# Cached attention decode on one core: the ring of tile slots moved to a multiple of 4096 bytes in each partition

## The chip, the cores and the metric

The kernel runs on one core of one Trainium2 chip. The metric is the device time of one execution in microseconds (us), the median of several runs. A profile belongs to one execution of its own; its span runs from the first to the last instruction.

## The reference

Two independent attention blocks, A and B, each decode one token against a cache; the outputs are put side by side.

```python
B, Sq, D = 8, 1, 1024
H, Sk, Dh = 32, 4096, 128
...
def _A_ref(x, k_cache, v_cache, wq, wo):
    q = (x @ wq).reshape(B, Sq, H, Dh).transpose(0, 2, 1, 3)
    scores = jnp.einsum("bhqd,bhkd->bhqk", q, k_cache) * (Dh ** -0.5)
    p = _softmax(scores, axis=-1)
    o = jnp.einsum("bhqk,bhkd->bhqd", p, v_cache)
    return o.transpose(0, 2, 1, 3).reshape(B, Sq, H * Dh) @ wo
...
return jnp.concatenate([a, b], axis=-1)
```

All is bfloat16. A cache of one block is 8 x 32 x 4096 x 128 numbers, 268 MB, and there are four: K and V of A and of B. Each number of a cache is used once.

## The kernel before, in words

The on-chip memory has 128 partitions. The kernel cuts each cache into tiles of 8 heads of one batch (`HQ = 8`): 8 x 4096 x 128 numbers, 8 MiB. A tile lies in the partitions as 128 rows of 65,536 bytes: each head has 16 partitions, and each partition 256 positions of 128 numbers (`T = 256`, `Dh = 128`). A block has 32 K tiles and 32 V tiles, so `NQ = 64` pairs of a K and a V tile in all. The weights wq and wo of a block are 8 MiB each and travel as tiles too.

**The ring.** `ring` (line 191) is one tensor of three tile slots, 3 x 65,536 bytes in each partition. The list `plan` (lines 271 to 275) says in which order the tiles are loaded and into which slot. K tiles take slots 0 and 1 in turn, V tiles take slot 2. A block's wq goes through slots 1 and 2; the last V tile and the two wo tiles use what is free. `load_tiles` (line 291) issues each load on SyncE's queue (SP) as soon as the operation that last used the slot has been issued to its engine; SP then waits on the chip for that operation to end (line 241 for cache tiles, line 233 for weights). The last wo comes in four pieces (`wo_cuts`, line 223: 20, 8, 3 and 1 of 32 heads' columns), so that the projection can begin on the first. The two inputs x are put into the start of slot 2 (line 479) by ScalarE's queue.

**The work on a K tile.** In four chunks of 64 positions (`CT = 64`, `NR = 4`): VectorE (DVE) multiplies the chunk in place by the query, which lies in `qbc` for all partitions (line 362); it adds the upper 64 numbers of each position to the lower 64 (line 367); TensorE adds four groups of 16 by matmuls with the identity `ident` (line 377) into PSUM; VectorE adds the last 16 into `s_sb` (line 385). After the fourth chunk come the maximum (lines 391 to 395), the exponential on ScalarE (line 397) into `pe`, and line 402, which spreads the probabilities over 8 columns (`PM`), of which each partition fills the one of its head.

**The work on a V tile.** TensorE multiplies `PM` with the V tile (line 414), 64 matmuls, half of them in the third and half in the fourth chunk of the next K tile. ScalarE copies the sum to `accS` (line 422), TensorE picks out the heads (line 431), and ScalarE stores them in `o_sb` (line 437). At the end come the division by the sums (line 451) and the two projections with wo (line 467), a copy (line 474) and the output.

**The order of the work.** It is written out by hand: each engine has a list of operations, filled by the loop at line 498, and each operation names what it waits for. Each `sb(...)` at lines 191 to 212 allocates a tensor in every partition; they lie one behind another in the order of these lines. Ahead of them lie four one-element constants that the framework allocates. Sizes per partition that matter here: `s_sb` 2 x 256 x 4 = 2048 bytes, `accS` 512 x 2 = 1024, `qst` 2 x 128 x 2 = 512, `ident` 128 x 2 = 256, `own_m` 8 x 4 x 4 = 128.

Of the kernel before, what the change touches and what calls it, by code (L numbers as in the profile page):

```python
# [8 lines left out]
BF16 = mybir.dt.bfloat16  # L9
FP32 = mybir.dt.float32  # L10
# [154 lines left out]
def _build_kernel(nc, caches, out):  # L165
    B, Sq, D = caches[0][0].shape
    _, H, Sk, Dh = caches[0][1].shape
# [6 lines left out]
    T = Sk // MP  # L174
# [12 lines left out]
    with es:  # L187
        sb = lambda name, shape, dt: es.enter_context(nc.sbuf_tensor(name, shape, dt))
        ps = lambda name, n=512: es.enter_context(nc.psum_tensor(name, [128, n], FP32))

        ring = sb("ring", [128, 3, T * Dh], BF16)
        ident = sb("ident", [128, 128], BF16)
        own_m = sb("own_m", [128, HQ, PH], FP32)
        own_h = sb("own_h", [128, HQ], BF16)
        half = sb("half", [128, 2], FP32)
        E = sb("E", [128, 4, MB + PH - 1], BF16)
        xT = sb("xT", [128, NC * DC * B], BF16)
        qT = sb("qT", [128, NC, H * B], BF16)
        qst = sb("qst", [128, 2, 128], BF16)
        qbc = sb("qbc", [128, 2, Dh], BF16)  # L200
        s_sb = sb("s_sb", [128, 2, T], FP32)
        rmax = sb("rmax", [128, 1], FP32)
        rtmp = sb("rtmp", [128, 32], FP32)
        ngm = sb("ngm", [128, 2], FP32)
        rsum = sb("rsum", [128, NQ], FP32)
        pe = sb("pe", [128, T], BF16)
        PM = sb("PM", [128, T, HQ], BF16)
        accS = sb("accS", [128, 512], BF16)
        o_sb = sb("o_sb", [128, NC * B * H], FP32)
        rl = sb("rl", [128, B], FP32)  # L210
        on_sb = sb("on_sb", [128, NC, B * H + H], BF16)
# [360 lines left out]
def bass_concat_heads__mha_block_cached__mha_block_cached__decode_kernel(  # L572
    nc, A_x, A_k_cache, A_v_cache, A_wq, A_wo, B_x, B_k_cache, B_v_cache, B_wq, B_wo, out,
):
    caches = [(A_x, A_k_cache, A_v_cache, A_wq, A_wo), (B_x, B_k_cache, B_v_cache, B_wq, B_wo)]
    _build_kernel(nc, caches, out)
# [28 lines left out]
```

## Time and profile before

| | us |
|---|---|
| median of 3 runs | 2563.58 (2563.41 to 2563.61) |
| span of the profiled execution | 2562.3 |
| DVE busy | 2170.4 (85%) |
| PE matmul busy | 1116.5 (44%) |
| ACT busy | 129.9 (5%) |
| time that the packets of the SP queue took, as a share of 16 DMA engines' span | 99.9% |

The profiled execution has its span beside no time of its own; it is 1.3 us below the median of the runs. PE is TensorE, PEld its weight loads, DVE VectorE, ACT ScalarE, POOL GpSimd, SP SyncE; SPq is SP's queue of DMA issues. A group row of the profile reads: line, engine, operation, output<-inputs, shapes, count, then busy time and mean ns of one, then the idle time of the engine ahead of it and what ended it. A row of the timeline reads: start and duration in us, engine, line, operation, and in brackets the idle time ahead of it with its releaser. A row of a tile's view gives the shortest, median and longest duration in ns. A row of waits gives the total, the count and the longest. A row of DMA issues gives the count, the size where it is one, and the time from issue to landing in us. A row of windows gives the stretch, its length, the busy time of PE, PEld, DVE, ACT and POOL with the count of instructions, TensorE's granted clock, the DMA engines' share and GB/s.

### The profile page before, as it was taken

The page shows a single profiled execution, that of the slowest core. Times are in us where ns is not written, and L with a number is a line of the kernel's source. Part 1 is how long each engine was busy: PE and PEld are TensorE (multiplying, and loading weights), DVE is VectorE, ACT ScalarE, POOL GpSimd, SP SyncE. Part 2 cuts the span into 40 slices and gives each one's busy share as a digit, 9 for nine tenths or more (in the row PEclk, how much of TensorE's full clock was granted, in tenths as well). Part 3 has the DMA queues.
Part 4 walks back from the last instruction along what each step waited for, and adds up shares of the span by engine and source line. Part 5 has one row for each costly group of instructions (what it writes and reads, how often), then busy time and mean ns, then how long its engine had stood idle before and what let it go on. Part 6 is the DMA issues. An engine that isn't in the chain of part 4 may idle for free.

```text
span 2562.3 us, 18889 instructions
## 1 busy us (share of the span) xinstructions
PE 1116.5 (44%) x7712; PEld 397.0 (15%) x7712; DVE 2170.4 (85%) x1042; ACT 129.9 (5%) x401; POOL 2.6 (0%) x15
## 2 busy tenths in 40 slices
PE   2443443443444444444434444444434434434434
PEld 0111111111111111111111111111111111111112
DVE  3898898898898898898898888988988988988983
ACT  1100000000000000000000000000000000000000
POOL 0000000000000000000000000000000000000000
PEclk8666676766767677767767767766767667666667
DMA  9999999999999999999999999999999999999999
GB/s 425 427 438 430 438 430 438 430 438 430 437 430 437 429 436 431 435 433 433 435 432 436 431 436 431 437 431 437 431 437 431 437 431 437 431 435 433 435 433 394
DMA packets 19552, 1107.49 MB, mean 432 GB/s; under 512 B 2184, under 2 KB 2248, under 8 KB 2520
## 3 DMA queue, kind: packets, MB, share of 16 engines
q1 hardware_dynamic: 19512, 1107.34, 99.9%
q8 instruction: 7, 0.11, 0.0%
q10 hardware_dynamic: 32, 0.03, 0.0%
q14 instruction: 1, 0.01, 0.0%
HBM read 1107.33 MB, written 0.03 MB: 432 GB/s over the span
## 4 chain that ended last, share of the span: by engine, by line
DMA 52%; DVE 28%; issue 16%; PE 4%; ACT 0%; another core or an unknown queue 0%; DVEq 0%; SPq 0%
DMA ring<-in_A_k_cache_dram 25%; DMA ring<-in_B_k_cache_dram 25%; DVE ring L362 10%; DVE ring L367 10%; PE red L377 4%; DVE s_sb L385 4%; DVE PM L402 3%; DMA ring<-in_B_wo_dram 2%; DVE rmax L391 1%; DVE rtmp L392 0%; ACT PM L323 0%; PE o L317 0%; DVEq L161 0%; DVE ngm L395 0%
## 5 line engine op out<-in xcount | busy, mean ns | idle before, releaser
L362 DVE TENSOR_TENSOR ring<-ring,qbc 128x8192 bf16<-128x8192 bf16 x256 | 1131.4, 4420 | 309.8 <-DMA ring<-in_A_k_cache_dram 156.7
L377 PE MATMUL red<-ring,ident 128*128 128x512 bf16 x2048 | 781.7, 551 | 1392.1 <-DVE ring L367 1392.1
L367 DVE TENSOR_TENSOR ring<-ring 128x4096 bf16<-128x4096 bf16 x256 | 581.8, 2273 | 0.0
L377 PEld LDWEIGHTS red<-ring,ident 128*128 128x128 bf16 x2048 | 239.3, 128 | 1843.0 <-DVE ring L367 1494.3
L385 DVE TENSOR_REDUCE s_sb<-red 128x64 f32<-128x1024 f32 x256 | 311.5, 1217 | 3.6 <-PE red L377 3.6
L414 PE MATMUL pv<-ring,PM 128*32 128x512 bf16 x4096 | 273.8, 414 | 4.7 <-DVE PM L402 4.7
L402 DVE TENSOR_TENSOR PM<-pe,own_h 128x2048 bf16<-128x2048 bf16 x64 | 146.2, 2284 | 0.7 <-ACT pe L397 0.7
L414 PEld LDWEIGHTS pv<-ring,PM 128*32 128x32 bf16 x4096 | 104.0, 104 | 187.7 <-issue 114.7
L351 ACT ACTIVATE qbc<-misc 128x128 bf16<-128x128 f32 x64 | 17.8, 278 | 1092.1 <-PE misc L349 1092.1
L397 ACT ACTIVATE pe<-s_sb,ngm 128x256 bf16<-128x256 f32 x64 | 32.5, 508 | 469.5 <-DVE ngm L395 469.5
L422 ACT ACTIVATE accS<-pv 128x512 bf16<-128x512 f32 x64 | 38.2, 597 | 352.4 <-PE pv L414 352.4
L431 PEld LDWEIGHTS o<-accS,E 128*32 128x32 bf16 x1024 | 31.3, 100 | 49.3 <-issue 48.1
L431 PE MATMUL o<-accS,E 128*32 128x32 bf16 x1024 | 38.1, 185 | 0.7 <-ACT accS L422 0.7
L437 ACT ACTIVATE o_sb<-o 32x32 f32 (+1 forms) x64 | 11.9, 186 | 449.8 <-PE o L431 441.9
L391 DVE TENSOR_REDUCE rmax<-s_sb 128x1 f32<-128x256 f32 x64 | 26.9, 420 | 2.2
L474 DVE CAST orow<-proj 128x256 bf16<-128x256 f32 x2 | 0.8, 424 | 27.2 <-PE proj L467 27.2
L337 DVE COPY qT<-misc 128x64 bf16<-128x64 bf16 x8 | 3.5, 436 | 18.8 <-PE misc L333 18.8
L344 ACT ACTIVATE qst<-qT 128x128 bf16 (+1 forms) x64 | 18.7, 293 | 1.9 <-DVE qT L337 1.9
L467 PE MATMUL proj<-ring,on_sb 128*32 128x256 bf16 x256 | 11.5, 351 | 16.6 <-DMA ring<-in_B_wo_dram 8.4
L392 DVE TENSOR_SCALAR rtmp<-half,rmax 128x32 f32<-128x32 f32 x64 | 15.4, 241 | 2.3
L395 DVE TRANSPOSE_TENSOR_REDUCE ngm<-rtmp 128x1 f32<-128x32 f32 x64 | 13.6, 212 | 2.2
L349 PE MATMUL misc<-ident,qst 128*128 128x128 bf16 x64 | 14.8, 231 | 0.9 <-ACT qst L344 0.9
(33 smaller groups left out, 65.5 us busy)
## 6 DMA issues: line engine op xcount, KB each, us to landing
ring<-in_B_wo_dram SPq DMA_DIRECT2D x1, 5120.0 KB, 32.9
ring<-in_B_wo_dram SPq DMA_DIRECT2D x1, 2048.0 KB, 37.4
ring<-in_B_wo_dram SPq DMA_DIRECT2D x1, 768.0 KB, 38.8
ring<-in_A_k_cache_dram SPq DMA_DIRECT2D x32, 40.0
ring<-in_A_v_cache_dram SPq DMA_DIRECT2D x32, 27.8
ring<-in_B_k_cache_dram SPq DMA_DIRECT2D x32, 39.8
ring<-in_B_v_cache_dram SPq DMA_DIRECT2D x32, 27.8
ring<-in_B_wo_dram SPq DMA_DIRECT2D x1, 256.0 KB, 39.0
```

The costliest lines, as they stand in the source:

```text
L344: return e.activation(qst[:, n % 2, :].rearrange("p (j m) -> p j m", m=MP), from_.unsqueeze(2).to_broadcast([128, HQ, MP]), ACTF.Copy)
L351: opQbc[n] = add("act", lambda e: e.activation(qbc[:, n % 2, :], misc[:, 0:Dh], ACTF.Copy), [opQb[n], _at(opMul, NR * (n - 2) + NR - 1)])
L362: opMul[s] = add("dve", lambda e: e.tensor_tensor(v, v, qbc[:, n % 2, :].unsqueeze(1).to_broadcast([128, CT, Dh]), ALU.mult), [opT[("k", n ...
L367: return add("dve", lambda e: e.tensor_tensor(v[:, :, 0:64], v[:, :, 0:64], v[:, :, 64:128], ALU.add), [opMul[s]])
L377: i = e.matmul(dst, ident[:], v[:, g, :, j, :], start=(j == 0), stop=(j == 3))
L385: opRed[s] = add("dve", lambda e: e.tensor_reduce(s_sb[:, n % 2, r * CT:(r + 1) * CT], red_ps[s % 2][:, :].rearrange("p (t w) -> p t w", w ...
L391: m = add("dve", lambda e: e.tensor_reduce(rmax[:], s_sb[:, n % 2, :], AX.X, ALU.max), [opRed[NR * n + NR - 1]])
L397: opExp[n] = add("act", lambda e, at: e.activation(pe[:], s_sb[:, n % 2, :], ACTF.Exp, bias=ngm[:, n % 2:n % 2 + 1], scale=scale, accum_ou ...
L402: opPM[n] = add("dve", lambda e: e.tensor_tensor(PM[:], pe[:].unsqueeze(2).to_broadcast([128, T, HQ]), own_h[:].unsqueeze(1).to_broadcast( ...
L414: i = e.matmul(pv_ps[32 * q:32 * (q + 1), :], PM[:, t:t + 4, :].rearrange("p t j -> p (t j)"), v[:, t * Dh:(t + 4) * Dh], start=(g == 0), ...
L422: opAcc[n] = add("act", lambda e: e.activation(accS[:], pv_ps[:], ACTF.Copy), [opPV[n], _at(opExt, n - 1)])
L431: x = e.matmul(to, E[:, i, PH - 1 - u:PH - 1 - u + MB], accS[:, i * 128 + H * u:i * 128 + H * (u + 1)], start=(i == 0 and u == 0), stop=(i ...
```

## The change

Five of the small tensors are allocated ahead of the ring in place of behind it, in a new order. Their sizes are 2048 + 1024 + 512 + 256 + 128 = 3968 bytes a partition. The tensors between the ring and their old places move up by what went ahead of them. No operation, size, wait or queue is changed.

```diff
-        ring = sb("ring", [128, 3, T * Dh], BF16)
+        s_sb = sb("s_sb", [128, 2, T], FP32)
+        accS = sb("accS", [128, 512], BF16)
+        qst = sb("qst", [128, 2, 128], BF16)
         ident = sb("ident", [128, 128], BF16)
         own_m = sb("own_m", [128, HQ, PH], FP32)
+        ring = sb("ring", [128, 3, T * Dh], BF16)
         own_h = sb("own_h", [128, HQ], BF16)
         half = sb("half", [128, 2], FP32)
         E = sb("E", [128, 4, MB + PH - 1], BF16)
         xT = sb("xT", [128, NC * DC * B], BF16)
         qT = sb("qT", [128, NC, H * B], BF16)
-        qst = sb("qst", [128, 2, 128], BF16)
         qbc = sb("qbc", [128, 2, Dh], BF16)
-        s_sb = sb("s_sb", [128, 2, T], FP32)
         rmax = sb("rmax", [128, 1], FP32)
         rtmp = sb("rtmp", [128, 32], FP32)
         ngm = sb("ngm", [128, 2], FP32)
         rsum = sb("rsum", [128, NQ], FP32)
         pe = sb("pe", [128, T], BF16)
         PM = sb("PM", [128, T, HQ], BF16)
-        accS = sb("accS", [128, 512], BF16)
```

## The prediction

> **What bounds the kernel now.** I read the page from the top: busy times, then the DMA parts.
>
> ```profile
> span 2562.3 us, 18889 instructions
> PE 1116.5 (44%) x7712; PEld 397.0 (15%) x7712; DVE 2170.4 (85%) x1042; ACT 129.9 (5%) x401; POOL 2.6 (0%) x15
> ...
> DMA  9999999999999999999999999999999999999999
> ...
> DMA packets 19552, 1107.49 MB, mean 432 GB/s; under 512 B 2184, under 2 KB 2248, under 8 KB 2520
> ...
> q1 hardware_dynamic: 19512, 1107.34, 99.9%
> ...
> HBM read 1107.33 MB, written 0.03 MB: 432 GB/s over the span
> ```
>
> No compute engine is full: VectorE (DVE) has 85%. The one DMA queue that carries the caches has packets in flight for 99.9% of the time of all 16 DMA engines, from the first slice to the last. That the queue never runs dry is seen from the issues and from who they waited for:
>
> ```profile
> SPq L241 <- PE pv L414: 1935.7, 62, 32.6
> ...
> SPq L241 <- PE red L377: 427.2, 63, 7.7
> ```
>
> ```profile
> ring<-in_A_k_cache_dram SPq DMA_DIRECT2D x32, 40.0
> ring<-in_A_v_cache_dram SPq DMA_DIRECT2D x32, 27.8
> ring<-in_B_k_cache_dram SPq DMA_DIRECT2D x32, 39.8
> ring<-in_B_v_cache_dram SPq DMA_DIRECT2D x32, 27.8
> ```
>
> The issuing engine waits for a slot to come free, but a K tile still takes 40 us from issue to landing and a V tile 27.8. What one tile needs by itself follows from one round (one K and one V tile) in the timeline:
>
> ```profile
> 1002.59 0.33 SPq L241 DMA_DIRECT2D ring<-in_A_v_cache_dram  x1
> 1009.78 0.33 SPq L241 DMA_DIRECT2D ring<-in_A_k_cache_dram  x1
> 1011.20 4.42 DVE L362 TENSOR_TENSOR ring<-ring,qbc 128x8192 bf16<-128x8192 bf16 x1 [4.79 <-DMA ring<-in_A_k_cache_dram]
> ...
> 1041.29 0.33 SPq L241 DMA_DIRECT2D ring<-in_A_v_cache_dram  x1
> 1048.80 0.33 SPq L241 DMA_DIRECT2D ring<-in_A_k_cache_dram  x1
> 1049.89 4.43 DVE L362 TENSOR_TENSOR ring<-ring,qbc 128x8192 bf16<-128x8192 bf16 x1 [4.78 <-DMA ring<-in_A_k_cache_dram]
> ```
>
> From one K landing to the next (1011.20 to 1049.89) is 38.69 us, 19.35 a tile. The V tile issued at 1002.59 lands 27.8 us later, at 1030.4, so it began to move at 1011.0, just when the K tile before it was in. The K tile issued at 1009.78 has its turn at 1030.4, 20.6 us after its issue; the next V tile, issued at 1041.29, has its turn at 1049.8, 8.5 us after. So the next transfer is always waiting in the queue, by 8.5 us at least, and VectorE stands idle 4.8 us in each round for the next K tile. The bound is the pace at which the queue writes tiles into the ring. Two issues far apart give that pace finely:
>
> ```profile
> 305.94 0.33 SPq L241 DMA_DIRECT2D ring<-in_A_v_cache_dram  x1
> ...
> 2473.24 7.04 SPq L241 DMA_DIRECT2D ring<-in_B_v_cache_dram  x2
> ```
>
> Between them are 56 rounds: 2167.30 / 56 = 38.702 us a round. A tile is 128 rows of 65,536 bytes, one row a partition; 16,777,216 bytes in 38.702 us are 433.5 GB/s. The 16 engines take 8 rows each of a tile, so an engine passes a row in 38.702 / 16 = 2.419 us.
>
> **The change part by part.** *The order of allocation.* The tensors put ahead of the ring hold 2048 (s_sb), 1024 (accS), 512 (qst), 256 (ident) and 128 (own_m) bytes a partition: 3968. With 128 bytes that already lie ahead (the four one-element constants; 32 bytes each is my reading of the sum, the profile shows no addresses), 3968 + 128 = 4096. So before, each slot, and with it each 64 KB row that the queue writes, starts 128 bytes past a multiple of 4096; after, on one, since the slots are 65,536 bytes apart. No instruction is added, removed or moved in any queue, no DMA has another size or order, and no wait changes. What can change is the price of an access.
>
> *The queue's writes.* These alone lie on the path, with nothing to hide them. The trace has no row that starts on a multiple of 4096, so the gain has to be bounded. If an unaligned start costs something, it costs it once a row (one broken block at its head and one at its tail), and it is part of what a row costs beyond its bytes. That can be read where rows are shorter: the last weight comes in four cuts whose rows have 40,960, 16,384, 6,144 and 2,048 bytes, all starting 128 past a multiple of 2048, and TensorE waits for them one by one.
>
> ```profile
> ring<-in_B_wo_dram SPq DMA_DIRECT2D x1, 5120.0 KB, 32.9
> ring<-in_B_wo_dram SPq DMA_DIRECT2D x1, 2048.0 KB, 37.4
> ring<-in_B_wo_dram SPq DMA_DIRECT2D x1, 768.0 KB, 38.8
> ...
> ring<-in_B_wo_dram SPq DMA_DIRECT2D x1, 256.0 KB, 39.0
> ```
>
> ```profile
> 2552.25 4.42 PE L467 MATMUL proj<-ring,on_sb 128*32 128x256 bf16 x80 [7.26 <-DMA ring<-in_B_wo_dram]
> 2557.06 1.10 PE L467 MATMUL proj<-ring,on_sb 128*32 128x256 bf16 x32 [0.38 <-DMA ring<-in_B_wo_dram]
> 2558.92 0.97 PE L467 MATMUL proj<-ring,on_sb 128*32 128x256 bf16 x16 [0.76 <-DMA ring<-in_B_wo_dram]
> ```
>
> The third cut came 2558.92 - 2557.06 = 1.86 us after the second. Its 786,432 bytes at 433.5 GB/s are 1.814 us, so 0.046 us is extra, for 8 row starts an engine where 64 KB rows would have 0.75: 0.046 / 7.25 = 6 ns a start. The second and third together: 2,883,584 bytes, 6.652 us at that pace, 6.67 measured: 0.018 us for 16 - 2.75 = 13.25 more starts, 1.4 ns a start. So a row start costs 1.4 to 6 ns, and what its misalignment costs is no more than all of it, and no less than nothing. The whole program has 64 + 64 cache tiles, two wq and one wo with full rows: 131 tiles x 8 = 1048 rows an engine. The ends are 0 and 1048 x 6 ns = 6.3 us of gain. For the forecast I stay by the reading over the longer stretch, 1.4 ns, and give half of it to the misalignment, since an aligned row has a start too: 0.7 ns x 1048 = **0.7 us**. That half is a choice, and the range does not rest on it.
>
> [...]
>
> *VectorE on the ring.* Line 362 and line 367 read and write the ring in place.
>
> ```profile
> L362 DVE TENSOR_TENSOR ring<-ring,qbc x256: 4412/4418/4427, 43.4 to 2507.9; 128x8192 bf16<-128x8192 bf16 x128
> ...
> L367 DVE TENSOR_TENSOR ring<-ring x256: 2248/2279/2291, 47.9 to 2513.4; 128x4096 bf16<-128x4096 bf16 x128
> ```
>
> The multiplications take 4412 to 4427 ns in both K slots and beside every DMA; every start moves by a multiple of 128 bytes (3968 = 31 x 128), so each stays on the same step within 128 bytes. I take nothing. A gain here would be hidden (VectorE would wait longer for the K tile). A loss is hidden by the 4.8 us of idle time a round.
>
> *The moved small tensors.* s_sb, accS, qst, ident and own_m move down; those between them and their old places move up. TensorE, ScalarE and VectorE read them as before. ScalarE has 5% and TensorE 44%, and all of it lies beside the queue; in the tail (the last 3.4 us after 2558.92) only line 467, the copy at line 474 and the output remain, which use the ring, on_sb and orow. on_sb and orow lie behind all moved tensors, so their places stay. Nothing.
>
> *Sum.* The profiled execution has a span of 2562.3 us; 2563.58 is the median of the runs, 1.3 us above it, which I leave as it is. 2563.6 - 0.7 = **2562.9 us**.
>
> **The rivals.** *The start cost goes wholly.* If the 6 ns a start are the broken blocks and nothing else, 1048 x 6 ns = 6.3 us go: 2557.3 us. For it: the queue has no slack, so all of it would show. Against it: the two cuts together give 1.4 ns a start, 1.5 us in all. [...] Chance 0.15.
>
> *Aligned rows are slower.* After the change the same row of every slot starts at the same place in its 4096-byte block, and all 16 engines begin their rows there together. If the start of such a row collided in the memory where one off the boundary does not, the price would be paid at the same place, once a row. Its size is unknown; by the nearest row, the 6 ns of a start, doubled starts give 1048 x 6 = 6.3 us: 2569.9 us. It decides from 0.2% on, 5.1 / 1048 = 4.9 ns a row. For it: nothing hides it either. Against it: before, too, the 16 engines start rows at one common offset (128), and the queue kept 433.5 GB/s. Chance 0.10.
>
> *VectorE becomes the bound.* A window of one round shows how far it is from that:
>
> ```profile
> 1041.29:1079.98 38.69, 16.57 (x113) 5.95 (x113) 33.81 (x17) 1.86 (x6) 0.00 (x0) 0.69 1.00 434
> ```
>
> VectorE is busy 33.81 of 38.69 us. If the new places of ring, qbc or s_sb slowed its instructions by over 4.8 / 33.8 = 14%, its round would set the pace. Twice the time for line 362 alone would add 4 x 4.42 = 17.7 us, 12.8 beyond the slack: 64 rounds x 12.8 = 819 us, 3383 us. Against it: 4412 to 4427 ns over both slots. Chance 0.03, and more likely near the threshold than at that end.
>
> *The change does not do what it says.* If something else lay ahead of the ring, it would start off the boundary as before and the time would be 2563.6. Chance 0.02.
>
> **How the numbers follow.** The forecast's own case, a gain or a loss below what can be told, has 0.70; it gives 2558.5 to 2565. A measurement of this kernel can tell about 0.2%, 5.1 us, from no change. Faster by more has the first rival, 0.15; slower by more has the second and third, 0.13; within are 0.70 and 0.02, together 0.72. The range reaches down to 2557.0, just under the whole start cost, and up to 2568.0, a little under the point from which the second rival decides; the slower cases beyond that, and the part of the first that goes below 2557.0, are the 2 in 10 left out.
>
> **What would show it.** Right: the K landings stay 38.70 us apart or come down by hundredths (0.7 ns x 16 rows = 0.011 us a round), lines 362 and 367 keep 4420 and 2273 ns, VectorE's idle time a round stays near 4.8 us, and the queue stays at 99.9%. The first rival shows as a round of 38.60 us and more than 434.5 GB/s, with the third cut of the last weight landing 1.82 us after the second. The second rival shows as a round of 38.80 us with VectorE's idle time grown by the same 0.1 us; the third as longer VectorE instructions and idle time gone. The prediction would be wrong if the pace inside a row, not its start, depended on where the row lies: then the short rows say nothing of it, and the gain or loss could be past both ends. [...]

## The result, and the profile after

The changed kernel takes 2559.15 us (median of 20 runs, 2558.95 to 2559.54) against 2563.56 us (2563.33 to 2563.76) for the kernel before on the same chips: 4.4 us less, a ratio of 0.9983 with a 95% interval of 0.9976 to 0.9989. The ranges of the runs do not touch.

The page of the kernel after, the lines that answer to those shown of before:

```profile
span 2558.0 us, 18889 instructions
...
PE 1117.0 (44%) x7712; PEld 396.9 (16%) x7712; DVE 2170.2 (85%) x1042; ACT 129.9 (5%) x401; POOL 2.6 (0%) x15
...
q1 hardware_dynamic: 19512, 1107.34, 99.9%
...
HBM read 1107.33 MB, written 0.03 MB: 433 GB/s over the span
```

The span fell by 4.3 us. No engine works less: DVE has 2170.2 us where it had 2170.4. The queue is as full as before and carries the same 19,512 packets, so it carries them faster. The issues of V tiles, the same two as before, give the pace:

```profile
305.27 0.33 SPq L241 DMA_DIRECT2D ring<-in_A_v_cache_dram  x1
...
2469.05 6.63 SPq L241 DMA_DIRECT2D ring<-in_B_v_cache_dram  x2
```

2163.78 us for 56 rounds are 38.639 us a round, where it was 38.702. The difference of 0.063 us over all 64 rounds is 4.0 us, so the gain lies evenly along the run and not at an end of it. VectorE's rows on the ring after the change, by tile:

```profile
L362 DVE TENSOR_TENSOR ring<-ring,qbc x256: 4412/4417/4427, 43.3 to 2503.7; 128x8192 bf16<-128x8192 bf16 x128
L367 DVE TENSOR_TENSOR ring<-ring x256: 2248/2278/2291, 47.7 to 2509.2; 128x4096 bf16<-128x4096 bf16 x128
```

Its group row before the change, and after it:

```profile
L362 DVE TENSOR_TENSOR ring<-ring,qbc 128x8192 bf16<-128x8192 bf16 x256 | 1131.4, 4420 | 309.8 <-DMA ring<-in_A_k_cache_dram 156.7 <-DMA ring<-in_B_k_cache_dram 153.1
```

```profile
L362 DVE TENSOR_TENSOR ring<-ring,qbc 128x8192 bf16<-128x8192 bf16 x256 | 1131.2, 4419 | 306.0 <-DMA ring<-in_A_k_cache_dram 154.9 <-DMA ring<-in_B_k_cache_dram 151.1
```

The durations are those of before to the nanosecond or two. The idle time went from 309.8 to 306.0 us: VectorE waits 3.8 us less for K tiles, which is nearly the whole gain, handed on from the queue.

The trace also has a record of each packet with its duration. A full row of 65,536 bytes is one packet. Counted by duration:

```
16768 packets of 65,536 bytes   to 2418 ns   2419-2422   2423-2431   longer
before                             2861         9566        4287        54
after                             16414          200          64        90
```

After the change nearly every row takes 2418 ns. Before, five in six took longer, nearly all of them by 1 to 13 ns. The mean fell from 2422.6 to 2419.0 ns; 3.6 ns over 1048 rows an engine are 3.8 us. So the queue paid something on most rows, and the change took it away.

### The profile page after: what moved, and what is told of

Its sections match the earlier page's. It is cut to its first block, busy times and chain, and to the rows that moved or that the text cites. A ratio compares the mean times of both kernels' runs of the same rounds, so it can differ in the third digit from the quotient of the medians.

```text
span 2558.0 us, 18889 instructions
## 1 busy us (share of the span) xinstructions
PE 1117.0 (44%) x7712; PEld 396.9 (16%) x7712; DVE 2170.2 (85%) x1042; ACT 129.9 (5%) x401; POOL 2.6 (0%) x15
## 3 DMA queue, kind: packets, MB, share of 16 engines
q1 hardware_dynamic: 19512, 1107.34, 99.9%
## 4 chain that ended last, share of the span: by engine, by line
DMA 52%; DVE 28%; issue 16%; PE 4%; ACT 0%; another core or an unknown queue 0%; DVEq 0%; SPq 0%
DMA ring<-in_A_k_cache_dram 25%; DMA ring<-in_B_k_cache_dram 25%; DVE ring L362 10%; DVE ring L367 10%; PE red L377 4%; DVE s_sb L385 4%; DVE PM L402 3%; DMA ring<-in_B_wo_dram 2%; DVE rmax L391 1%; DVE rtmp L392 0%; ACT PM L323 0%; PE o L317 0%; DVEq L161 0%; DVE ngm L395 0%
## 5 line engine op out<-in xcount | busy, mean ns | idle before, releaser
L362 DVE TENSOR_TENSOR ring<-ring,qbc 128x8192 bf16<-128x8192 bf16 x256 | 1131.2, 4419 | 306.0 <-DMA ring<-in_A_k_cache_dram 154.9
```

The costliest lines, as they stand in the source:

```text
L362: opMul[s] = add("dve", lambda e: e.tensor_tensor(v, v, qbc[:, n % 2, :].unsqueeze(1).to_broadcast([128, CT, Dh]), ALU.mult), [opT[("k", n ...
```

## The experiments

Each kernel was timed against the kernel before on the same chip, whose median was 2563.61 to 2563.66 us. "Off by" is the distance of a slot's start from a multiple of 4096 bytes, which is also its distance from the 256-byte boundary below it, but for 256 itself. The profile shows no addresses: like the prediction's 128, these distances are the author's reading of the tensors' sizes, each taken up to a multiple of 32 bytes as the prediction took the four constants; no run shows them. The four theories at the start: A, what a row pays grows with the distance of its start from the 256-byte boundary below it, by an estimate from the 4.4 us at 128 bytes 1.1 us at 32 and 7.7 us at 224; B, a row that starts off the 256-byte block pays one price; C, the 4096-byte block counts; D, it is not the ring but the new places of the five small tensors.

**The alignment undone, the tensors left in their new places (off by 128).**

```diff
 own_m = sb("own_m", [128, HQ, PH], FP32)
+rtmp = sb("rtmp", [128, 32], FP32)
 ring = sb("ring", [128, 3, T * Dh], BF16)
```

> The five tensors stay ahead of the ring and rtmp (128 bytes) goes ahead too, so that each slot starts 128 bytes past a multiple of 4096 again. If the start of the ring is what counts (theories A, B and C): the gain is undone, 2563.6 us, a round of 38.70 us. If the new places of the five small tensors brought the gain (theory D): 2559.2 us, 38.64 us a round.

Measured: 2563.59 us (2563.28 to 2563.80, 11 runs). Its issues:

```profile
305.99 0.33 SPq L241 DMA_DIRECT2D ring<-in_A_v_cache_dram  x1
...
2473.28 6.71 SPq L241 DMA_DIRECT2D ring<-in_B_v_cache_dram  x2
```

2167.29 / 56 = 38.702 us, the round of before. The whole gain is gone, so theory D falls: the ring's start is the cause.

**Aligned to 256 bytes and not to 4096 (off by 256).** From the kernel before, one line is moved:

```diff
+own_m = sb("own_m", [128, HQ, PH], FP32)
 ring = sb("ring", [128, 3, T * Dh], BF16)
 ident = sb("ident", [128, 128], BF16)
-own_m = sb("own_m", [128, HQ, PH], FP32)
```

> Only own_m (128 bytes) goes ahead of the ring, so that each slot starts 256 bytes past a multiple of 4096; the other four tensors stay behind it. If a row pays for a start off a 256-byte block (theories A and B): it is aligned, 2559.2 us, 38.64 us a round. If it pays for blocks of 4096 bytes (theory C), or if the places of the small tensors count (theory D): 2563.6 us, 38.70 us.

Measured: 2559.15 us (2559.00 to 2559.65, 11 runs), the time of the change.

```profile
305.47 0.33 SPq L241 DMA_DIRECT2D ring<-in_A_v_cache_dram  x1
...
2469.16 7.79 SPq L241 DMA_DIRECT2D ring<-in_B_v_cache_dram  x2
```

38.637 us a round. Theory C falls: 256 bytes are enough, and one tensor ahead of the ring does what five did.

**Off by 32 and by 224.** From the kernel after, small tensors are added ahead of the ring:

```diff
# off by 32
+own_h = sb("own_h", [128, HQ], BF16)
 ring = sb("ring", [128, 3, T * Dh], BF16)
# off by 224
+rtmp = sb("rtmp", [128, 32], FP32)
+own_h = sb("own_h", [128, HQ], BF16)
+half = sb("half", [128, 2], FP32)
+rmax = sb("rmax", [128, 1], FP32)
 ring = sb("ring", [128, 3, T * Dh], BF16)
```

> As after the change, with own_h ahead as well: each slot starts 32 bytes past a multiple of 4096. [...] If any start off the block costs the same (theory B), or off 4096 (theory C): 2563.6 us. Theory D: 2559.2 us.

> As after the change, with rtmp, own_h, half and rmax ahead as well: each slot starts 224 bytes past a multiple of 4096. [...] Theories B and C (one price for any start off the block): 2563.6 us. Theory D: 2559.2 us.

Measured: 2564.87 us (2564.59 to 2565.01) at 32 and 2564.78 us (2564.55 to 2564.89) at 224, 11 runs each. The issues at 32 bytes:

```profile
305.89 0.33 SPq L241 DMA_DIRECT2D ring<-in_A_v_cache_dram  x1
...
2474.18 7.83 SPq L241 DMA_DIRECT2D ring<-in_B_v_cache_dram  x2
```

2168.29 / 56 = 38.720 us. Theory A falls: over the aligned ring 32 bytes off cost 5.7 us and 224 bytes 5.6 us. Theory B is nearly right; there is one price for any start off the block, but 32 and 224 both cost 1.2 to 1.3 us more than 128, which neither theory had.

**Off by 64.**

```diff
+own_h = sb("own_h", [128, HQ], BF16)
+half = sb("half", [128, 2], FP32)
 ring = sb("ring", [128, 3, T * Dh], BF16)
```

> As after the change, with own_h and half ahead as well: each slot starts 64 bytes past a multiple of 4096. If every start off a 256-byte block has a price, with a second one for a start off 64 bytes (as the two runs at 32 and 224 bytes suggest, both 1.2 us over the run at 128): as at 128, 2563.6 us. If the price falls step by step with the distance from 128 bytes: between, 2564.2 us. [...]

Measured: 2563.79 us (2563.53 to 2564.03, 11 runs), 0.2 us over the run at 128. So 64 belongs to 128, not to 32: of the four distances tried, the two that are multiples of 64 pay 4.4 to 4.6 us, the two that are not pay 5.6 to 5.7.

**Once a row, or along it? Two DMAs of half rows for each cache tile.** In the kernel after (off by 0) and in the kernel before (off by 128) alike:

```diff
-return e.dma_start(to, whole[...].rearrange("(p x) -> p x", p=128))
+return e.dma_start(to[:, lo:lo + T * Dh // 2], whole[...].rearrange("(p x) -> p x", p=128)[:, lo:lo + T * Dh // 2])
...
-opT[(kind, n)] = load_cache(to, n, 1 if kind == "k" else 2, key, [dep])
+for lo in (0, T * Dh // 2):
+    opT[(kind, n)] = load_cache(to, n, 1 if kind == "k" else 2, key, [dep], lo)
```

> The ring as after the change, but each cache tile comes in two DMAs of 32 KB rows, so 1024 more row starts an engine and 128 more completion messages. By the predicted price of a row start, 1.4 to 6 ns: 1.4 to 6.1 us more, 2560.6 to 2565.3 us. If a start costs more than that, the time shows how much.

> The same two DMAs of 32 KB rows a tile, with the ring as before the change (128 bytes off). If the misalignment is paid once a row start: twice the 4.4 us, so 8.8 us over the run with aligned half rows. If it is paid along the row, by its length: 4.4 us over it.

Measured: 2564.62 us (2564.46 to 2564.84, 11 runs) aligned, within what was expected, and 2573.72 us (2573.19 to 2574.03, 5 runs) off by 128. The issues of the two, aligned first:

```profile
305.74 0.81 SPq L241 DMA_DIRECT2D ring<-in_A_v_cache_dram  x2
...
2474.31 7.30 SPq L241 DMA_DIRECT2D ring<-in_B_v_cache_dram  x4
```

```profile
306.87 0.80 SPq L241 DMA_DIRECT2D ring<-in_A_v_cache_dram  x2
...
2482.86 6.62 SPq L241 DMA_DIRECT2D ring<-in_B_v_cache_dram  x4
```

Rounds of 38.724 and 38.857 us: 0.133 us apart, where whole rows gave 0.063. The difference of the two medians is 9.1 us, twice the 4.4 of whole rows, so **the misalignment is paid once for each row start**. And a start has its own price: 1024 more of them an engine (with 128 more completion messages) cost 5.5 us aligned, 5.3 ns each, and 10.1 us unaligned (2573.72 - 2563.61), 9.9 ns each. The messages are in these prices: in the packet records of before and after a message of 4 bytes takes 9 ns, so 128 of them an engine are an estimated 1.2 us, which leaves 4.2 ns for an aligned start and 8.8 ns for an unaligned one.

**Half of the tiles aligned.** Slot 2 starts 128 bytes later, once with the ring as after (V off, K aligned), once with the ring as before (K off, V aligned):

```diff
-ring = sb("ring", [128, 3, T * Dh], BF16)
+ring = sb("ring", [128, 3 * T * Dh + 64], BF16)
+at_slot = (0, T * Dh, 2 * T * Dh + 64)
...
-to, key = ring[:, w, :], ("t", w)
+to, key = ring[:, at_slot[w]:at_slot[w] + T * Dh], ("t", w)
...
```

> As after the change, but slot 2 alone starts 128 bytes later, so that nearly all V rows are off the block and the K rows on it. If each row pays for itself: about half of the 4.4 us, 2561.4 us. If one unaligned stream puts the whole queue off its pace: 2563.6 us.

> The ring as before the change (128 bytes off a multiple of 4096), but slot 2 starts 128 bytes later and so on a 256-byte block: K rows off the block, V rows on it, the mirror of the run with V alone off, which came 0.8 us over the aligned ring and not 2.2. If half of the rows off cost little whichever half it is, because aligned rows make up for it (the write side has slack when aligned): 2559.9 us. If K rows carry most of the price: 4.4 - 0.8 = 3.6 us over the aligned ring, 2562.8 us. If each row pays alike after all: 2561.4 us.

Measured: 2559.93 us (2559.75 to 2560.21) with V off, 2560.04 us (2559.86 to 2560.42) with K off, 11 runs each. Neither of the two expectations of the first run held: half the rows off cost 0.8 us, not 2.2 and not 4.4. Its mirror shows that it does not matter which half: 0.9 us.

The trace has the completion messages of each tile. From the last message of one tile to the last of the next, a tile took in the mean (tiles that landed from 300 to 2480 us; for three tiles of four see the next run):

| | a tile off by 128 takes | an aligned tile takes |
|---|---|---|
| all off (before) | 19.351 us | |
| V off, K aligned | 19.356 us | 19.295 us |
| K off, V aligned | 19.352 us | 19.296 us |
| three tiles of four off | 19.352 us | 19.293 us |
| all aligned (after) | | 19.320 us (K 19.314, V 19.326) |

The slow tile is the one that is written off the block (19.351 to 19.356 us), in whichever slot it lies. An aligned tile is faster next to unaligned ones (19.293 to 19.296 us) than among aligned ones (19.320 us).

**Three tiles of four off.** From the run with K off: slots 0 and 2 off by 128, slot 1 aligned.

```diff
-at_slot = (0, T * Dh, 2 * T * Dh + 64)
+at_slot = (0, T * Dh + 64, 2 * T * Dh + 128)
```

> As the run with K alone off, but slots 0 and 2 off the block by 128 bytes and slot 1 on it: every second K tile aligned, three of four tiles off. If each row pays alike: 3/4 of 4.4, 2562.5 us. If aligned tiles make up for others, up to a floor set elsewhere: a tile then takes on the mean what the writes take, (19.301 + 3 x 19.351) / 4 = 19.339 us against the floor of 19.319, 128 x 0.020 = 2.5 us over the aligned ring, 2561.7 us.

Measured: 2561.57 us (2561.38 to 2561.78, 11 runs), 2.4 us over the aligned ring, by the issues

```profile
305.78 0.33 SPq L242 DMA_DIRECT2D ring<-in_A_v_cache_dram  x1
...
2471.54 7.68 SPq L242 DMA_DIRECT2D ring<-in_B_v_cache_dram  x2
```

38.674 us a round. The price over the shares of unaligned tiles runs 0, 0.8 to 0.9 (half), 2.4 (three quarters), 4.4 us (all): flat at first and then steep. Equal shares would give 2.2 and 3.3. The theory that fits was stated before this run: the writes, when aligned, are a little faster than something else that sets a floor, so aligned tiles make up for unaligned ones until their slack is used. The table of tiles above bears it out: an aligned tile takes 19.295 us between unaligned ones, but 19.32 where all are aligned. So the price of an unaligned start is (19.351 - 19.295) / 8 = 7.0 ns, and the floor at 19.32 us leaves (19.351 - 19.320) / 8 = 3.9 ns of it to be gained. Over 1048 rows 7.0 ns would be 7.3 us, still less than the 9.1 us of the half rows, so a floor does not let a price along the row explain those. The last quarter costs 2563.59 - 2561.57 = 2.0 us for 256 row starts an engine, 7.9 ns each, near that full price too.

**The reads moved instead of the writes**, and both.

```diff
 ...
-whole[bass.ds(at(n % (B * HB) * size, size), size)]...
+whole[bass.ds(at(n % (B * HB) * size, size) + (64 if n % (B * HB) < B * HB - 1 else 0), size)]...
```

> The ring as after the change, but each cache tile (all but the last of a cache) is read 64 numbers (128 bytes) further on in the cache, so that the reads start off a 256-byte block and the writes on it; what is computed is attention over shifted tiles. [...] By the price found for writes: 4.4 us, 2563.6 us. If only writes pay: 2559.2 us.

> The ring as before the change and the cache tiles read 128 bytes further on, as in the run with the reads off: reads and writes both start 128 bytes past a 256-byte block; what is computed is attention over shifted tiles. If the price comes from the shift between where a row is read and where it is written: none here, 2559.2 us. If each side pays by itself and they add: 2568 us. If the slower side sets the pace: 2563.6 us.

Measured: 2559.15 us (2559.01 to 2560.17) with the reads off alone, 2563.67 us (2563.45 to 2563.91) with both off, 11 runs each. The issues with the reads off alone:

```profile
305.30 0.33 SPq L241 DMA_DIRECT2D ring<-in_A_v_cache_dram  x1
...
2469.22 7.83 SPq L241 DMA_DIRECT2D ring<-in_B_v_cache_dram  x2
```

38.641 us. Reading 128 bytes off the block costs nothing that shows, where the price of the writes would be 4.4 us, and it neither adds to nor takes from what the writes cost. So it is the place of the write, not that of the read and not the shift between the two.

## Why the prediction was right, and where it was off

*The bound.* Right. Of 4.4 us, 4.0 are the pace of the queue in the 64 rounds, and VectorE's idle time fell along with it.

*The writes alone can change.* Right: with the alignment undone in the new order of tensors the gain was 0.0 us.

*A start off the boundary is paid once a row.* Right, by the half rows: 9.1 us for twice the starts against 4.4. That the price comes from a broken block at the row's head and one at its tail was the author's guess; no run shows it.

*The ends of the price, 0 to 6 ns a row.* They held what was gained, 4.41 us / 1048 = 4.2 ns, but not the price of the misalignment itself, 7.0 ns a start by the tiles' landings: the upper end held because of a floor that the prediction did not have. The time lies in the range, and in the bounds of the forecast's own case (2558.5 to 2565), near its lower end. That case was a change too small to be told, within 5.1 us; the 20 runs of each of the two kernels spread over 0.6 us at most, so 4.4 us can be told well, and the time lay in those bounds because they were wide.

*The size chosen inside them, 0.7 ns.* Wrong by a factor of six, and here a step failed: "the second and third together ... 1.4 ns a start". An unaligned start costs 9.9 ns by the half rows, seven times that (8.8 ns without the messages). The reading took the times at which TensorE began for the times at which the cuts landed. In the trace's records of completion messages, the last message of the second cut came 4.900 us after that of the first and the last of the third 1.861 us later, 6.761 us, where TensorE's starts gave 6.67: TensorE took up the first cut 0.09 us later after its message than the second and third. By the messages, (6.761 - 6.652) / 13.25 = 8.2 ns a start, from the same run. The single step from the second to the third cut, 6 ns, had no such fault and lay nearer, though one step scatters between runs: by the messages it took 1.82 to 1.85 us in the four runs with the whole ring aligned and 1.84 to 1.89 us in the seven with every slot off, so the two overlap. Both steps together took 6.66 to 6.68 and 6.72 to 6.81 us in these runs, which do not; in the run with three tiles of four off, where the last weight lies aligned, they took 6.72. After the change the cuts show the gain too:

```profile
2547.98 4.49 PE L467 MATMUL proj<-ring,on_sb 128*32 128x256 bf16 x80 [6.90 <-DMA ring<-in_B_wo_dram]
2552.74 1.10 PE L467 MATMUL proj<-ring,on_sb 128*32 128x256 bf16 x32 [0.27 <-DMA ring<-in_B_wo_dram]
2554.55 0.98 PE L467 MATMUL proj<-ring,on_sb 128*32 128x256 bf16 x16 [0.72 <-DMA ring<-in_B_wo_dram]
```

From the second to the third are 1.81 us, where it was 1.86; the prediction named 1.82 as the sign of the first rival. It is a weak sign by itself: in the run at 256 bytes, aligned too, the same step took 1.85 us.

*Half of the start's price to the misalignment.* Nearly right as a share: unaligned 9.9 ns, aligned 5.3, so 4.5 of 9.9 go, or 4.5 of 8.8 without the messages.

*The first rival, the start cost goes wholly.* Its time, 2557.3, was 1.85 us too low; its place and kind were right. Its round of 38.60 us is what two aligned tiles between unaligned ones would take (2 x 19.295 = 38.59); with all tiles aligned the floor holds the round at 38.64. And an aligned start still has a price, 4.2 to 5.3 ns.

*The second rival, aligned rows slower*, and *the third, VectorE slower*: neither came. The rows took 2418 ns, the shortest that was common before, and lines 362 and 367 stayed where they were.

What stays open: what sets the floor of 38.64 us a round that the aligned queue runs at, how much of the 9.1 us of the half rows a floor took, and why starts off a 64-byte boundary cost 1.2 us more than those on one. That reads 128 bytes off the block cost nothing that shows may mean that they pay nothing, or that what they pay lies under that floor.

## What to carry to other kernels

Where a DMA queue is the bound and never dry, put the destination of its rows on a multiple of 256 bytes in the partition; a tensor of 128 bytes moved ahead was enough here, and 4096 gave no more (2559.15 us both). It was worth some 4 ns a row start for each engine here, so little for long rows (0.17% at 64 KB, 4.4 of 2563.6 us) and twice the share at half the length (0.35%, 9.1 of 2573.7 us). To read a start's price from a profile, take the times of landings, not those at which an engine took the data up, and take a long stretch or several runs: steps of hundredths of a microsecond scatter by as much as they tell.

## What the runs showed of the hardware

At the four distances tried, the price of an unaligned write start did not go by how far off the 256-byte block it was, but by whether it was off (4.4 to 4.6 us at 64 and 128) and whether it was off a 64-byte boundary as well (5.6 to 5.7 us at 32 and 224). Prices of rows did not add up over the run: half of the rows off cost a fifth of the whole price, 0.8 to 0.9 of 4.4 us, since the aligned tiles, at 19.295 us in place of 19.32, made up for the others at 19.35.
